# Splitting the queries and keys of both heads once and copying the parts on chip into the doubled layout

## Chip, cores and metric

One core of a Trainium2 chip runs the whole kernel. The metric is the device time of one execution in microseconds.

## What is computed

Three layers follow each other. Only the first is touched by the change; it is cut to its core here, the others are told in a sentence.

```python
# q, k, v: (4 batches, 8 heads, 576 positions, 64), float32
def _attn_ref(q, k, v, tau):
    scores = (1.0 / np.sqrt(64)) * np.matmul(q, k.transpose(0, 1, 3, 2))
    thresh = np.max(scores, axis=-1, keepdims=True) - tau
    scores = np.where(scores >= thresh, scores, -1e9)
    attn = np.exp(scores - np.max(scores, axis=-1, keepdims=True))
    attn = attn / (np.sum(attn, axis=-1, keepdims=True) + 1e-09)
    return np.matmul(attn, v)
```

The heads are then put side by side (512 channels). A mixing layer adds a low-rank product over positions (U, V) and a two-layer channel network with 2048 hidden units. A last layer sends each token to one of eight experts (512 to 1024 to 512); a gate decides whether a token takes a fresh expert or that of the token before it.

## The kernel before

**Splitting.** All large products are made from float32r operands that are split in two: a high part, which is the value rounded by a ScalarE copy, and a low part, which is the value minus the high part.

**Pairs of heads.** The heads are worked on in pairs: 16 pairs, four for each of the four batches. For a pair, `load_pair` makes four tiles: `qs`, `kh`, `kl` (128 partitions by 1216 columns each) and `v`. The 1216 columns hold both heads side by side, with the last 64 positions of the second head placed where the last group of rows needs them. A head has only 64 channels, so the 128 partitions are used twice: `qs` has the high part of the queries on partitions 0 to 63 and the low part on 64 to 127; `kh` has the high part of the keys on both halves, `kl` the low part on both halves. One matmul against `kh` (L293) and one against `kl` (L295) then add up all four products. This is the doubled layout; the host lays out the input tensor with the same data on both halves (`in_qk_dram`, 128 partitions).

**Loading a pair before the change.** For every pair but the first, four pieces are loaded: two of the keys (576 and 640 columns) and two of the queries (608 each), all on 128 partitions (SyncE's DMA queue, L263). ScalarE writes the high part of a piece (L269 for keys, L272 for queries, with the scale), then the low part of the keys is written on 128 partitions (L270) and that of the queries on partitions 64 to 127 alone (L274, VectorE). The engine of L270 is GpSimd for pairs 1 to 7 and VectorE for pairs 8 to 15. The pieces go through a tile `raw` with three buffers; `qs`, `kh`, `kl` and `v` have two buffers each, so the tiles of pair i+1 come free when pair i-1 has been used. The first pair is cut in six pieces so that it can start early.

**Attention of batch 0 alone.** `attention_alone(0)` runs 36 half groups, nine for each pair. A half group is 128 query rows of one head: scores on TensorE (L293, L295), their maximum on VectorE (`peak`, L328), a limit (L332), the exponential on ScalarE (L339), and masking with the row sum on VectorE (L343). Transposes (L391), their evictions on ScalarE (L392), the product with `v` (L410 to L414) and a short chain of mixing steps follow. `load_pair` of the next pair is called in the second group of a pair and is advanced by one step (one `yield` in the loader) for each half group.

**Converting weights.** Beside it, `convert` turns the 64-bit weights of the channel network to float32: a load (L184), a ScalarE cast (L192), a VectorE join (L199) and a store to a DRAM buffer `wdram` (L223). `load_w` reads them back (L609), ScalarE writes their high part (L612) and GpSimd or VectorE the low part (L614).

**Batches 1 to 3.** The attention of batch b is interleaved with the channel network of batch b-1 (`channel`, L630 to L650). Here `load_pair` of the next pair is called as a whole at the start of a pair. After the last attention come the last channel network and the experts.

**Order of work.** Each engine runs its instructions in a fixed order, and so does SyncE's queue, from which all these DMAs are issued: a DMA that has to wait for a semaphore holds up those behind it. The order is laid down at build time by a planner that takes instructions in the order of the program as far as its own estimates say that they are ready.

Of the kernel before, what the change touches and what calls it, by code (L numbers as in the profile page):

```python
# [8 lines left out]
F32 = mybir.dt.float32  # L9
F32R = mybir.dt.float32r  # L10
# [4 lines left out]
AF = mybir.ActivationFunctionType  # L15
ALU = mybir.AluOpType
# [4 lines left out]
B, H, S, D = 4, 8, 576, 64  # L21
# [7 lines left out]
QKW = 1216  # L29
# [54 lines left out]
def attention_channel_moe(ctx, tc, qk, vv, tau, umat, vrep, wch, wgl, wexp, consts, out):  # L84
    nc = tc.nc
    pe, dve, act, pool, sp = nc.tensor, nc.vector, nc.scalar, nc.gpsimd, nc.sync
# [10 lines left out]
    t8 = cp.tile([128, 4], F32, name="t8")  # L97
# [55 lines left out]
    ap = att.enter_context(tc.tile_pool(name="ap", bufs=2, side="right"))  # L153
# [79 lines left out]
    def scalars():  # L233

        sp.dma_start(out=t8[:, 0:1], in_=tau)

        dve.tensor_scalar(out=t8[:, 1:2], in0=t8[:, 0:1], scalar1=NEGTAU, scalar2=0.125, op0=ALU.is_ge, op1=ALU.mult)
        dve.tensor_scalar(out=t8[:, 2:3], in0=t8[:, 1:2], scalar1=0.0, scalar2=BIG, op0=ALU.is_equal, op1=ALU.mult)
        dve.tensor_scalar(out=t8[:, 0:1], in0=t8[:, 0:1], scalar1=0.0, scalar2=t8[:, 2:3], op0=ALU.max, op1=ALU.add)

    def load_pair(b, hp, later=None):

        i = b * NPAIR + hp
        v = ap.tile([128, VW], F32, tag="v", name=f"v{i}")
        qs = ap.tile([128, QKW], F32R, tag="qs", name=f"qs{i}")
        kh = ap.tile([128, QKW], F32R, tag="kh", name=f"kh{i}")
        kl = ap.tile([128, QKW], F32R, tag="kl", name=f"kl{i}")

        cuts = ((0, 0, 128), (1, 0, S), (0, 704, 832), (1, S, QKW), (0, 128, 704), (0, 832, QKW)) if i == 0 else (
            (1, 0, S), (1, S, QKW), (0, 0, 608), (0, 608, QKW))  # L250
        eng = dve if i == 0 or b > 1 else pool
        def steps():
            for n, (kq, c0, c1) in enumerate(cuts):
                c = slice(c0, c1)
                nm = f"raw{i}_{n}"
                if (i, n) == (0, 1):
                    x = mlp.tile([128, S], F32, tag="yr", name=nm, bufs=2)
                elif i == 0 and c1 - c0 == 128:
                    x = mlp.tile([128, 512], F32, tag="wr", name=nm, bufs=WR)
                else:  # L260
                    x = ap.tile([128, 640], F32, tag="raw", name=nm, bufs=3)
                x = x[:, :c1 - c0]
                sp.dma_start(out=x, in_=qk[i][:, kq, c])  # L263
                if (i, n) == (0, 0):
                    scalars()
                if (i, n) == (0, 3):
                    sp.dma_start(out=cst, in_=consts)
                if kq:
                    act.activation(kh[:, c], x, AF.Copy)  # L269
                    eng.tensor_tensor(out=kl[:, c], in0=x, in1=kh[:, c].bitcast(F32), op=ALU.subtract)  # L270
                else:
                    act.activation(qs[:, c], x, AF.Copy, scale=t8[:, 1:2])  # L272
                    lo, hi, xl = qs[64:128, c], qs[64:128, c].bitcast(F32), x[64:128]
                    dve.scalar_tensor_tensor(out=lo, in0=xl, scalar=t8[64:128, 1:2], in1=hi,  # L274
                                             op0=ALU.mult, op1=ALU.subtract)
                yield
            sp.dma_start(out=v, in_=vv[i])

        if later is None:
            for _ in steps():  # L280
                pass
        else:
            later.append(steps())
        return qs, kh, kl, v
# [213 lines left out]
    def attention(b):  # L498
        prev = None
        nxt = load_pair(b, 0)  # L500
        for hp in range(NPAIR):
            inp = nxt
            if hp + 1 < NPAIR:
                nxt = load_pair(b, hp + 1)
            for g in range(5):
                fr = front(b, hp, g, inp)
                yield 1.0
                if prev is not None:
                    yield from with_chain(back(*prev))
                prev = (b, hp, g, inp, fr)  # L510
        yield from with_chain(back(*prev))
        while CHAIN:
            yield link()

    def attention_alone(b):

        pend, debt, loads = [], 0.0, []
        inps = {0: load_pair(b, 0)}
        seq = [(hp, g, h) for hp in range(NPAIR) for g in range(5) for h in range(1 if g == 4 else 2)]
        groups = {}  # L520
# [768 lines left out]
```

## Time and profile before

| | |
|---|---|
| median of 3 runs | 1056.27 us (1054.12 to 1058.85) |
| profiled execution, its own time | 1052.12 us |
| its span, first to last instruction | 1050.4 us |
| mean granted TensorE clock | 0.994 |
| TensorE busy | 1011.7 us (96%) |
| VectorE busy | 714.9 us (68%) |
| ScalarE busy | 576.9 us (55%) |
| GpSimd busy | 133.8 us (13%) |

PE is TensorE's matmul side and PEld its weight loads, DVE is VectorE, ACT is ScalarE, POOL is GpSimd, SP is SyncE, and SPq is its queue. L274 is line 274 of the kernel. The shares are means over stages that differ, so the rows further down go by stretches of the span.

### The profile page before, as it was taken

What the parts mean: (1) busy time and instruction counts of PE and PEld (TensorE: products, weight loads), DVE (VectorE), ACT (ScalarE), POOL (GpSimd) and SP (SyncE); (2) the same over time, 40 slices, a digit from 0 to 9 for tenths busy, and PEclk for the clock granted to TensorE, in tenths of its full rate; (3) what the DMA queues carried; (4) which work ended last, traced back from release to release, by engine and by line L of the source; (5) the groups of instructions that cost most, each with busy time, mean ns of one, the idle gap of its engine ahead of it and who ended that gap; (6) DMA issues with size and microseconds to landing.
All of it is one profiled execution on the core that took longest, in us unless ns stands there. A gap on an engine that the chain in (4) does not pass through costs nothing. (4 is left out here: it accounts for less than half of the span.)

```text
span 1050.4 us, 19186 instructions
## 1 busy us (share of the span) xinstructions
PE 1011.7 (96%) x7081; PEld 896.7 (85%) x7081; DVE 714.9 (68%) x1742; ACT 576.9 (55%) x1216; POOL 133.8 (13%) x114
## 2 busy tenths in 40 slices
PE   8788899999999999999999999999999999999996
PEld 5566789888888999888889988999998988989984
DVE  7889776775776677677767755583367855566673
ACT  6788676674756466474646546422354344455462
POOL 1331032220100000000000000003420321111100
PEclk9999999999999999999999999999999999999998
DMA  6554577763423132142312102353145475456650
GB/s 214 201 157 144 168 251 232 256 217 100 132 71 114 64 93 83 60 132 71 113 55 66 52 31 71 106 201 105 47 160 182 145 262 171 151 189 206 205 181 16
DMA packets 57926, 143.80 MB, mean 137 GB/s; under 512 B 7069, under 2 KB 7837, under 8 KB 57824
## 3 DMA queue, kind: packets, MB, share of 16 engines
q1 hardware_dynamic: 54464, 132.27, 38.5%
q0 software_dynamic: 3360, 10.23, 3.0%
q8 instruction: 57, 0.93, 0.4%
q14 instruction: 45, 0.37, 0.1%
HBM read 124.65 MB, written 18.61 MB: 136 GB/s over the span
## 5 line engine op out<-in xcount | busy, mean ns | idle before, releaser
L630 PE MATMUL l<-uh,w0h 128*128 128x256 f32 (+1 forms) x512 | 158.7, 310 | 0.5 <-DVE L L686 0.2
L647 PE MATMUL l<-hh,w1h 128*128 128x256 f32 (+1 forms) x512 | 156.8, 306 | 0.0
L631 PE MATMUL l<-ul,w0h 128*128 128x256 f32 (+1 forms) x512 | 152.9, 299 | 0.0
L632 PE MATMUL l<-uh,w0l 128*128 128x256 f32 (+1 forms) x512 | 152.7, 299 | 0.0
L649 PE MATMUL l<-hh,w1l 128*128 128x256 f32 (+1 forms) x512 | 152.5, 298 | 0.0
L648 PE MATMUL l<-hl,w1h 128*128 128x256 f32 (+1 forms) x512 | 152.3, 298 | 0.0
L339 ACT ACTIVATE p<-s,st 128x576 f32<-128x576 f32 x144 | 104.3, 741 | 57.0 <-DVE st L328 56.7
L1039 ACT ACTIVATE eh<-ew 128x512 fp32r<-128x512 f32 x160 | 94.3, 628 | 71.6 <-PE el L1155 43.1
L1040 DVE TENSOR_TENSOR el<-ew,eh 128x512 fp32r<-128x512 f32 x160 | 106.6, 692 | 37.7 <-ACT eh L1039 36.3
L343 DVE SCALAR_TENSOR_TENSOR p<-s,st,p 128x576 f32<-128x576 f32 x144 | 114.1, 813 | 11.9 <-ACT p L339 8.3
L328 DVE TENSOR_REDUCE st<-s 128x1 f32<-128x576 f32 x144 | 105.5, 751 | 15.3 <-PE s L295 13.5
L392 ACT ACTIVATE ptt<-tp 128x512 f32<-128x512 f32 (+1 forms) x192 | 91.2, 494 | 39.1 <-PE tp L391 38.1
L293 PE MATMUL s<-kh,qs 128*128 128x288 f32 x320 | 97.3, 323 | 9.7 <-DVE p L343 6.4
L650 DVE TENSOR_TENSOR yT<-l,yT 128x256 f32<-128x256 f32 (+1 forms) x128 | 58.2, 454 | 70.4 <-PE l L649 69.8
L614 POOL TENSOR_TENSOR w1l<-wr,w1h 128x512 fp32r<-128x512 f32 x24 | 32.1, 1359 | 540.8 <-ACT w1h L612 520.9
L630 PEld LDWEIGHTS l<-uh,w0h 128*128 128x128 f32 x512 | 97.4, 190 | 3.9 <-ACT yr L699 2.0
L647 PEld LDWEIGHTS l<-hh,w1h 128*128 128x128 f32 x512 | 97.1, 190 | 2.9 <-issue 2.2
L631 PEld LDWEIGHTS l<-ul,w0h 128*128 128x128 f32 x512 | 97.4, 190 | 0.4
L648 PEld LDWEIGHTS l<-hl,w1h 128*128 128x128 f32 x512 | 97.0, 189 | 0.6
L632 PEld LDWEIGHTS l<-uh,w0l 128*128 128x128 f32 x512 | 97.2, 190 | 0.2
L649 PEld LDWEIGHTS l<-hh,w1l 128*128 128x128 f32 x512 | 96.9, 189 | 0.2 <-issue 0.2
L391 PE MATMUL tp<-cst,p 128*128 128x128 f32 x576 | 92.5, 276 | 3.9 <-ACT ptt L392 3.5
(450 smaller groups left out, 2308.9 us busy)
## 6 DMA issues: line engine op xcount, KB each, us to landing
ew<-in_wexp_dram SPq DMA_DIRECT2D x80, 512.0 KB, 4.5
wr<-wdram SPq DMA_DIRECT2D x128, 256.0 KB, 2.9
cr<-in_wch_dram SPq DMA_DIRECT2D x32, 512.0 KB, 4.9
raw<-in_qk_dram SPq DMA_DIRECT2D x30, 304.0 KB, 3.3
wdram<-w SPq DMA_DIRECT2D x32, 256.0 KB, 3.0
v<-in_vv_dram SPq DMA_DIRECT2D x16, 352.0 KB, 3.3
raw<-in_qk_dram SPq DMA_DIRECT2D x16, 320.0 KB, 3.1
raw<-in_qk_dram SPq DMA_DIRECT2D x17, 288.0 KB, 3.3
```

The lines of the kernel that those rows point to most:

```text
L293: pe.matmul(s["t"][:, h, :288], lhsT=qs[:, qc:qc + 128], rhs=kh[:, k0:k0 + 288], start=(j == 0), stop=False)
L328: dve.tensor_reduce(out=self.st[:, 0, h:h + 1], in_=self.t[h], axis=AX.XY, op=ALU.max, negate=True)
L339: act.activation(self.halves(h), self.t[h], AF.Exp, bias=self.st[:, 0, h:h + 1])
L343: dve.scalar_tensor_tensor(out=p, in0=self.t[h], scalar=self.st[:, 1, h:h + 1], in1=p, op0=ALU.is_ge, op1=ALU.mult, accum_out=self.rvs[:, ...
L630: pe.matmul(pm, lhsT=w1h[:, wk], rhs=uh[:, k, o:o + n], start=(k == 0), stop=False)
L631: pe.matmul(pm, lhsT=w1h[:, wk], rhs=ul[:, k, o:o + n], start=False, stop=False)
L632: pe.matmul(pm, lhsT=w1l[:, wk], rhs=uh[:, k, o:o + n], start=False, stop=(k == 3))
L647: pe.matmul(pm, lhsT=w2h[:, wd], rhs=hh[:, o:o + n], start=(f == f0), stop=False)
L648: pe.matmul(pm, lhsT=w2h[:, wd], rhs=hl[:, o:o + n], start=False, stop=False)
L649: pe.matmul(pm, lhsT=w2l[:, wd], rhs=hh[:, o:o + n], start=False, stop=(f == f0 + 3))
L1039: act.activation(hi, x, AF.Copy)
L1040: dve.tensor_tensor(out=lo, in0=x, in1=hi.bitcast(F32), op=ALU.subtract)
```

## The change

All pairs but the first are loaded by a new generator, `packed`. It loads each of keys and queries once, with the first head on partitions 0 to 63 and the second on 64 to 127 (two DMAs of 64 partitions by 640 columns from `in_qk_dram`). ScalarE writes the high part to a second `raw` tile, the low part is written in place over the loaded tile, both on 128 partitions by 640 columns. Twelve DMAs from SBUF to SBUF, of 64 partitions by 576 or 640 columns, then put these parts into `kh`, `kl` (four each) and `qs` (four). The first pair keeps its six pieces. What `qs`, `kh` and `kl` hold in the end is the same, as are all instructions that read them.

```diff
-        cuts = (...) if i == 0 else ((1, 0, S), (1, S, QKW), (0, 0, 608), (0, 608, QKW))
+        cuts = ((0, 0, 128), (1, 0, S), (0, 704, 832), (1, S, QKW), (0, 128, 704), (0, 832, QKW))
         eng = dve if i == 0 or b > 1 else pool
...
+        def packed():
+
+            for kq in (1, 0):
+                x, hi = (ap.tile([128, 640], F32, tag="raw", name=f"raw{i}_{kq}{t}", bufs=3) for t in "xh")
+                sp.dma_start(out=x[:64], in_=qk[i][:64, kq, 0:640])
+                sp.dma_start(out=x[64:], in_=qk[i][64:, kq, S:QKW])
+                if kq:
+                    act.activation(hi.bitcast(F32R), x, AF.Copy)
+                    eng.tensor_tensor(out=x.bitcast(F32R), in0=x, in1=hi, op=ALU.subtract)
+                    parts = [(t, y, r) for t, y in ((kh, hi), (kl, x)) for r in (0, 64)]
+                else:
+                    act.activation(hi.bitcast(F32R), x, AF.Copy, scale=t8[:, 1:2])
+                    dve.scalar_tensor_tensor(out=x.bitcast(F32R), in0=x, scalar=t8[:, 1:2], in1=hi,
+                                             op0=ALU.mult, op1=ALU.subtract)
+                    parts = [(qs, hi, 0), (qs, x, 64)]
+                yield
+                for t, y, r in parts:
+                    t, c = t[r:r + 64].bitcast(F32), 576 if kq else 640
+                    sp.dma_start(out=t[:, :c], in_=y[:64, :c])
+                    sp.dma_start(out=t[:, c:], in_=y[64:, 640 - QKW + c:])
+                yield
+            sp.dma_start(out=v, in_=vv[i])
+
+        steps = steps if i == 0 else packed
```

## Rows read from the trace of the kernel before

**Rows 1.** Busy time of each engine by stretch of the span.

```profile
core 0: us, PE busy (x) PEld busy (x) DVE busy (x) ACT busy (x) POOL busy (x), PEclk, DMA share, GB/s
27.00:52.00 25.00, 19.59 (x122) 14.30 (x124) 21.60 (x56) 19.25 (x41) 8.80 (x8) 0.93 0.58 196
52.00:75.00 23.00, 20.37 (x141) 14.87 (x139) 20.40 (x53) 19.91 (x43) 5.73 (x5) 1.00 0.51 159
75.00:98.00 23.00, 20.32 (x143) 14.82 (x142) 20.88 (x50) 18.05 (x39) 3.74 (x3) 1.00 0.52 162
...
102.00:146.00 44.00, 39.54 (x280) 34.25 (x280) 32.45 (x75) 31.83 (x71) 10.32 (x9) 0.96 0.59 184
146.00:188.00 42.00, 40.94 (x310) 36.79 (x309) 30.00 (x65) 29.06 (x60) 12.11 (x10) 1.00 0.76 249
...
297.00:461.00 164.00, 162.18 (x1231) 146.51 (x1224) 120.03 (x300) 95.87 (x204) 0.00 (x0) 1.00 0.28 89
```

**Rows 2.** Groups by line and shape from 0 to 110 us, of DVE, ACT and POOL.

```profile
line engine op names shapes xcount | busy us, mean ns | idle before us <-releasers
L343 DVE SCALAR_TENSOR_TENSOR p<-s,st,p 128x576 f32<-128x576 f32 x37 | 29.9, 813 | 4.3 <-ACT p L339 3.9
L274 DVE SCALAR_TENSOR_TENSOR qs<-raw,t,qs 64x608 fp32r<-64x608 f32 x10 | 9.8, 976 | 0.3
...
L272 ACT ACTIVATE qs<-raw,t 128x608 fp32r<-128x608 f32 x10 | 8.1, 814 | 0.6 <-DMA raw<-in_qk_dram 0.6
...
L269 ACT ACTIVATE kh<-raw 128x640 fp32r<-128x640 f32 x6 | 4.4, 737 | 1.6 <-DMA raw<-in_qk_dram 1.6
L269 ACT ACTIVATE kh<-raw 128x576 fp32r<-128x576 f32 x6 | 4.1, 684 | 1.8 <-issue 1.0 <-DMA raw<-in_qk_dram 0.8
...
L270 POOL TENSOR_TENSOR kl<-raw,kh 128x640 fp32r<-128x640 f32 x5 | 8.2, 1646 | 1.2 <-ACT kh L269 1.2
L270 POOL TENSOR_TENSOR kl<-raw,kh 128x576 fp32r<-128x576 f32 x5 | 7.5, 1490 | 16.4 <-ACT kh L269 16.3
```

**Rows 3.** One line's or tile's instructions over the whole span: ns least/median/most.

```profile
L274 DVE SCALAR_TENSOR_TENSOR qs<-raw,t,qs x34: 351/851/2095, 4.4 to 564.1; 64x608 fp32r<-64x608 f32 x30, 64x128 fp32r<-64x128 f32 x2, 64x576 fp32r<-64x576 f32 x1, 64x384 fp32r<-64x384 f32 x1
...
L199 DVE SCALAR_TENSOR_TENSOR w<-cr,top x32: 673/683/1733, 31.9 to 242.5; 128x512 int32<-128x512 int32 x32
```

**Rows 4.** Timeline of POOL and DVE around 75 and 99 us (start, duration).

```profile
75.59 2.92 POOL L270 TENSOR_TENSOR kl<-raw,kh 128x576 fp32r<-128x576 f32 x2 [2.95 <-ACT kh L269]
...
77.06 2.10 DVE L274 SCALAR_TENSOR_TENSOR qs<-raw,t,qs 64x608 fp32r<-64x608 f32 x1
...
99.04 3.39 POOL L270 TENSOR_TENSOR kl<-raw,kh 128x576 fp32r<-128x576 f32 x2 [0.58 <-ACT kh L269]
...
99.51 1.49 DVE L199 SCALAR_TENSOR_TENSOR w<-cr,top 128x512 int32<-128x512 int32 x1
```

**Rows 5.** DMA issues: KB each, median us from issue to landing.

```profile
raw<-in_qk_dram SPq DMA_DIRECT2D x17, 288.0 KB, 3.3
ydram<-yr SPq DMA_DIRECT2D x16, 256.0 KB, 3.2
ydram<-yr SPq DMA_DIRECT2D x4, 128.0 KB, 2.4
```

**Rows 6.** The stores out of tile w: us to landing, least/median/most.

```profile
DMA to landing us min/median/max: 2.0/3.0/5.5
```

**Rows 7.** Timeline around the loading of pair 1: SPq, ACT, PE.

```profile
9.71 0.33 SPq L263 DMA_DIRECT2D raw<-in_qk_dram  x1
...
11.62 0.86 SPq L263 DMA_DIRECT2D raw<-in_qk_dram  x2
...
13.59 0.67 ACT L269 ACTIVATE kh<-raw 128x576 fp32r<-128x576 f32 x1
...
28.38 0.40 PE L293 MATMUL s<-kh,qs 128*128 128x288 f32 x1 [0.35 <-DVE p L343]
```

**Rows 8.** Pair 2: last low part, first scores; batch 0: last scores; pair 6.

```profile
41.79 0.85 DVE L274 SCALAR_TENSOR_TENSOR qs<-raw,t,qs 64x608 fp32r<-64x608 f32 x1
...
54.55 0.40 PE L293 MATMUL s<-kh,qs 128*128 128x288 f32 x1
...
97.25 0.30 PE L295 MATMUL s<-kl,qs 128*128 128x288 f32 x1
...
152.76 0.85 DVE L274 SCALAR_TENSOR_TENSOR qs<-raw,t,qs 64x608 fp32r<-64x608 f32 x1 [0.19 <-ACT qs L272]
...
188.67 0.38 PE L293 MATMUL s<-kh,qs 128*128 128x288 f32 x1
```

**Rows 9.** Waits of SP's queue from 0 to 100 us: total, times, longest.

```profile
SPq L223 <- DVE w L199: 22.3, 5, 7.5
SPq L263 <- DVE qs L274: 12.8, 6, 3.6
SPq L263 <- POOL kl L270: 12.1, 7, 3.0
```

**Rows 10.** A converted weight on its way: store issue, load issue, low part, first use.

```profile
128.97 0.32 SPq L223 DMA_DIRECT2D wdram<-w  x1
...
132.34 0.32 SPq L609 DMA_DIRECT2D wr<-wdram  x1
...
133.83 1.30 POOL L614 TENSOR_TENSOR w0l<-wr,w0h 128x512 fp32r<-128x512 f32 x1 [1.23 <-ACT w0h L612]
...
137.87 0.36 PE L630 MATMUL l<-uh,w0h 128*128 128x256 f32 x1
```

More of the change, by code (lines that the diff above doesn't have):

```diff
@@ L247, in load_pair @@
         kl = ap.tile([128, QKW], F32R, tag="kl", name=f"kl{i}")
-        cuts = ((0, 0, 128), (1, 0, S), (0, 704, 832), (1, S, QKW), (0, 128, 704), (0, 832, QKW)) if i == 0 else (
-            (1, 0, S), (1, S, QKW), (0, 0, 608), (0, 608, QKW))
+        cuts = ((0, 0, 128), (1, 0, S), (0, 704, 832), (1, S, QKW), (0, 128, 704), (0, 832, QKW))
         eng = dve if i == 0 or b > 1 else pool
@@ L255, in steps @@
                 nm = f"raw{i}_{n}"
-                if (i, n) == (0, 1):
+                if n == 1:
                     x = mlp.tile([128, S], F32, tag="yr", name=nm, bufs=2)
-                elif i == 0 and c1 - c0 == 128:
+                elif c1 - c0 == 128:
                     x = mlp.tile([128, 512], F32, tag="wr", name=nm, bufs=WR)
@@ L263, in steps @@
                 sp.dma_start(out=x, in_=qk[i][:, kq, c])
-                if (i, n) == (0, 0):
+                if n == 0:
                     scalars()
-                if (i, n) == (0, 3):
+                if n == 3:
                     sp.dma_start(out=cst, in_=consts)
```

## The prediction

> **What bounds the kernel now.** I read the busy time by stretch first, then the loader's own groups, then single instructions around the loads.
>
> By stretch [rows 1] the span falls in two. From about 102 us on, TensorE is the bound: 162.2 of 164 us busy between 297 and 461 us, 40.9 of 42 between 146 and 188. Work taken from other engines there can give back only the holes, 1.8 us and 1.1 us in these two stretches. Before 98 us it is different. From 27 to 98 us DVE is busy for 21.6 + 20.4 + 20.9 = 62.9 of 71 us (89%), ACT for 57.2 (81%), PE for 60.3 (85%, with room). In this stretch a half group passes DVE, ACT and DVE again, and DVE has least room: it sets the pace, together with the hand-overs to ACT. The DVE group L343 shows 4.3 us of idle time, 3.9 of it behind ACT's exponential [rows 2]. So what the change does to DVE, and to a lesser degree to ACT, in the first 110 us is what can shorten the run. Five pairs (1 to 5) are split in that time: ten query pieces of L274 and ten POOL subtractions [rows 2].
>
> **The change part by part.**
>
> *Query low parts on DVE (removed and replaced).* Two L274 of 64x608 at 0.851 us median [rows 3] become one of 128x640. Using 128 partitions in place of 64 costs nothing: L343, of the same kind with as many columns but on 128 partitions, takes 0.813 us for 576 [rows 2]. With some 32 more columns I take 0.88 us. Saved for a pair: 1.70 - 0.88 = 0.82 us, for five pairs 4.1 us.
>
> *High parts on ACT.* Four copies, 0.684 + 0.737 + 2 x 0.814 = 3.05 us [rows 2], become two: 0.737 for the keys and about 0.84 for the queries (0.814 with 32 columns more, at 53 ns for 64 columns as between the two key pieces). Saved: 1.47 us for a pair, 7.3 us for five.
>
> *Key low parts.* On POOL 1.490 + 1.646 = 3.14 us become 1.65 [rows 2]; 1.49 us are saved for a pair. POOL is idle most of the time, so that by itself is worth nothing. But two DVE instructions that ran beside L270 took 2.10 us where the median is 0.851, and 1.49 us where it is 0.683 [rows 3, 4]: 2.1 us lost to DVE. With half of the POOL work I take half of that back, 1.0 us; ends 0 and 2.1. In batches 2 and 3 the same subtraction is DVE's and gets cheaper by about half, in a stretch that PE bounds: nothing.
>
> So DVE gets 5.1 us in the stretch that it paces. How much becomes time? At least nothing (the pieces may already sit in DVE's idle time, 8.1 of 71 us), at most all 5.1. I take half, **-2.6 us**: the splits can be placed freely, so a part of them fills waits, but with 89% busy not all can. ACT's 7.3 us I count as nothing in the forecast; a rival counts them.
>
> *Loads from the input.* Four DMAs of 128 partitions become four of 64, with 64 x 640 x 4 bytes = 160 KB each; the loaded bytes of a pair fall from 1.19 to 0.63 MiB. Off the path.
>
> *Copies from SBUF to SBUF (added).* Twelve for a pair, 180 in all, each 144 or 160 KB on 64 partitions; 1.78 MiB a pair. No row shows such a copy. One issue costs SP 0.43 us (two in 0.86 [rows 7]), so 5.2 us of SP time for a pair. The landing: the nearest rows are stores out of SBUF, 2.4 us for 128 KB from 64 partitions and 3.2 us for 256 KB from 128 [rows 5], and 2.0 to 5.5 us with a median of 3.0 for the stores of w [rows 6]. I take 3.0 with ends 2.0 and 5.5. In those two rows of ydram half the data takes three quarters of the time, so two halves one after the other would be dearer than one whole, but they are issued 0.43 us apart and overlap. The Trainium skill speaks against this layout: in "SBUF — State Buffer", section "Can I just issue two DMAs to hit both halves?", it says that two DMAs on the two halves of the partitions run hardly faster than one after the other, and in "The DMA port swizzle" that 64 partitions reach half of the ports. By that rule the twelve copies would move at the rate of half the ports, and the estimate from its 218 GB/s is 8.6 us of transfer for a pair; no row here shows it.
>
> *Is the new chain early enough?* The new order is load, ACT, POOL, copy, land, and for the queries once more, with a second wait in between: `raw` has three buffers, so the high part of the queries needs a buffer that the key copies have freed. For pair 1, with ACT starting at 13.6 us as now [rows 7]: high part done at 14.3, POOL at 15.9. The four high copies are issued by 16.0 and land at 16.0 + L; then ACT 0.84, DVE 0.88, four copies 1.7, and the last lands at 19.4 + 2L, plus up to 1.6 us if ACT and DVE are each busy with one instruction. With L = 3.0 that is 25.4 to 27.0 us, with 5.5 it is 30.4 to 32.0, with 2.0 it is 23.4. The pair's first scores run at 28.38 [rows 7]. So the price is 0 to 3.6 us; I take **+0.5**. Pairs from 2 on have cover: the last low part of pair 2 is done at 42.64 and its scores start at 54.55, for pair 6 it is 153.61 and 188.67 [rows 8]. The two landings and the issues fit in 11.9 us. They even start sooner, since the split no longer waits for the old `kh` to be free; only the copies do. Without that cover a pair would cost one landing, 3.0 us.
>
> *SP's queue.* Behind a waiting copy stand the loads and stores of the converted weights; they in turn feed ACT's casts (L192) and the low parts (L614). SP already waits much, 22.3 us in all for the join and 12.1 us behind POOL's `kl` up to 100 us [rows 9], so its own time is not short. After 110 us I take 0 with ends -2 and +2, the size of the holes of PE [rows 1].
>
> **Sum.** 1052.12 (profiled execution) - 2.6 + 0.5 = 1050.0 us. The median of the runs is 4.15 us above the profiled execution, so the forecast against it is **1054.2 us**, 0.2% faster. A measurement of this kernel tells about 0.5% from no change, 5.3 us, so I call this no difference.
>
> **The rivals.**
>
> *Hidden anyway.* The splits already fill waits, and the gain of DVE turns into idle time: 1056.3, or 1056.8 with the late start of pair 1. For it: 8.1 us of DVE idle time between 27 and 98 us. Against it: DVE is the busiest engine there.
>
> *Both engines count.* A half group needs DVE, ACT and DVE in turn, and ACT is also busy for 81%; a piece on either delays the exponential. Then all 5.1 us of DVE count and half of ACT's 7.3: 8.8 us, 1052.12 - 8.8 = 1043.3, or 1047.5 beside the median. For it: DVE's waits for the exponential [rows 2]. Against it: PE has 5.4 + 2.6 + 2.7 = 10.7 us of idle time from 27 to 98 us [rows 1], so PE itself would soon bound the stage.
>
> *SP's queue holds up the weights (slower).* A copy of a low part waits at the head of SP's queue until POOL is done (1.65 us), and the query copies wait for a landing (3.0): 4.65 us in which nothing behind them is issued. A converted weight has little room: its low part ends at 133.83 + 1.30 = 135.13 us and PE uses it at 137.87 [rows 10], 2.7 us. Each of pairs 2 to 5, loaded while weights are converted, would then cost 4.65 - 2.7 = 1.95 us, 7.8 us in all: 1050.0 + 7.8 = 1057.8, or 1062.0 beside the median. It decides from a hold of 2.7 us on, if planner and chip disagree on when the copies are ready. For it: the holds already there [rows 9] and a DMA share of 0.76 between 146 and 188 us [rows 1], which lengthens landings. Against it: the low parts of pairs 2 to 5 fall before the weights are needed. The rule on halves quoted above would bring the same result, since it lengthens every landing.
>
> *The change not doing what it says* is not among them: fewer and wider instructions are in the diff itself.
>
> **How the numbers follow.** Forecast 0.37, hidden anyway 0.18, both engines 0.24, SP's queue 0.21. Forecast and hidden lie within 0.5%: same 0.55; faster by over 0.5% (below 1051.0) 0.24; slower (above 1061.6) 0.21. The range takes in the values of all rivals and some of their spread: 1046 to 1064.
>
> **What would show it.** In the profile after: one L274-like instruction of 128x640 for a pair at about 0.88 us, ACT copies of 640 columns at 0.74 and 0.84, POOL subtractions of 1.65 us; DVE busy 4 to 5 us less up to 110 us and the last scores of batch 0 some 2 to 3 us earlier than 97.5 [rows 8]; first scores of pair 1 near 28; copies that land in 2.4 to 4 us; unchanged busy time and about the same holes of PE after 110 us. I am wrong if the end of the first stage moves by over 5 us either way, if DVE or PE wait for `qs`, `kh` or `kl`, if PE has new holes before L630 and L647, or if the granted clock falls in a new hole.

## The result and the profile after

The changed kernel takes 1066.87 us (median of 4 runs, 1065.62 to 1067.93) beside 1055.9 us for the kernel before (4 runs, 1054.12 to 1058.85). The ratio is 1.0100 with a 95% interval of 1.0078 to 1.0122: about 11 us, or 1.0%, slower. The forecast was 1054.2 us, and the range ended at 1064.

The profiled execution took 1065.62 us, its span is 1063.8 us, and the granted clock is 0.994 as in the profile of before, so the loss isn't one of clock. First the page of after, its lines of busy time and the group of the matmul with `w0l` (L655, before L632; lines behind the loader have moved by 23):

```profile
PE 1019.3 (96%) x7080; PEld 898.0 (84%) x7081; DVE 697.0 (66%) x1719; ACT 562.5 (53%) x1186; POOL 123.8 (12%) x107
...
L655 PE MATMUL l<-uh,w0l 128*128 128x256 f32 (+1 forms) x512 | 152.3, 299 | 3.5 <-POOL w0l L637 3.3
```

The relief came: VectorE is busy 697.0 us in place of 714.9, ScalarE 562.5 in place of 576.9, GpSimd 123.8 in place of 133.8. It was not turned into time. A matmul lasts as long as before (299 ns for this group). Busy time by stretch, the columns of [rows 1]:

```profile
27.00:52.00 25.00, 20.63 (x130) 13.58 (x131) 18.35 (x48) 17.25 (x38) 4.25 (x5) 1.00 0.74 206
52.00:75.00 23.00, 18.83 (x132) 14.41 (x131) 16.91 (x48) 18.12 (x39) 2.83 (x2) 1.00 0.67 175
75.00:98.00 23.00, 20.66 (x140) 14.70 (x139) 18.56 (x51) 16.86 (x38) 2.20 (x2) 1.00 0.78 216
```

From 27 to 98 us VectorE has 53.8 us of work where it had 62.9 [rows 1], and it stands idle instead. Not all of the difference is relief: by 110 us the queries of three pairs have been split in place of five [rows 2], so some of that work has only been put off. TensorE does no more than before. How far it falls behind is best counted in matmuls, since a matmul that starts late by less than its own length leaves no idle time. Three stretches, 0 to 110, 110 to 188 and 188 to 297 us (PE busy and its count, granted clock, DMA share, GB/s), of before and then of after:

```profile
0.00:110.00 110.00, 93.37 (x589) 0.98 0.58 185
110.00:188.00 78.00, 73.92 (x547) 0.98 0.66 210
188.00:297.00 109.00, 106.75 (x812) 1.00 0.51 162
```

```profile
0.00:110.00 110.00, 93.14 (x578) 1.00 0.76 206
110.00:188.00 78.00, 71.30 (x515) 0.98 0.77 231
188.00:297.00 109.00, 103.63 (x764) 1.00 0.76 221
```

After is 11 matmuls behind by 110 us, 32 more by 188 and 48 more by 297: 91, and at 164 us for 1231 matmuls [rows 1] that is 12.1 us. It agrees with the first scores of pair 8, at 309.79 us in place of 297.23. From there on the distance stays, up to 13.4 us between the two spans; these two profiles lie a little further apart than the medians. The last scores of batch 0 run at 101.74 us in place of 97.25 [rows 8], but the first matmul of the channel network runs at 117.7 us in both. Nearly nine tenths of the loss come after 110 us, where I had put 0, and what falls behind there is the first layer of the channel network: from 110 to 188 us 152 of its matmuls run (L653 to L655) in place of 199.

Two waits of after tell of two places. Up to 110 us VectorE's maximum waits for scores (total, times, longest; before, then after). Between 110 and 290 us TensorE waits for a low part of weights, which it never did before:

```profile
DVE st L328 <- PE s L295: 4.8, 9, 1.2
```

```profile
DVE st L351 <- PE s L318: 16.2, 14, 5.3
```

```profile
PEld l L655 <- POOL w0l L637: 5.2, 7, 1.2
...
PE l L655 <- POOL w0l L637: 3.3, 6, 0.9
```

The second wait is small beside the loss: 3.3 us before matmuls, 5.2 us before their weight loads, while the 80 matmuls lost after 110 us are worth 10.7 us at the rate above. The rest isn't traced to a wait.

**Place 1: pairs that start late.** Pair 1, in the timeline of after (start, duration, engine, line):

```profile
20.49 0.60 SPq L283 DMA_DIRECT2D raw_0x<-in_qk_dram  x1
...
28.34 0.85 ACT L289 ACTIVATE raw_0h<-raw_0x,t 128x640 fp32r<-128x640 f32 x1
...
31.05 0.55 SPq L297 DMA_DIRECT2D qs<-raw_0x  x1
...
34.98 0.40 PE L316 MATMUL s<-kh,qs 128*128 128x288 f32 x1
...
35.81 0.76 DVE L351 TENSOR_REDUCE st<-s 128x1 f32<-128x576 f32 x1 [5.27 <-PE s L318]
```

The second half of the queries is loaded behind the eight key copies, and the first scores run at 34.98 us in place of 28.38 [rows 7]. Pair 2 has the same shape, the whole chain from its first load on:

```profile
32.28 0.49 SPq L282 DMA_DIRECT2D raw_1x<-in_qk_dram  x1
...
40.24 0.73 ACT L285 ACTIVATE raw_1h<-raw_1x 128x640 fp32r<-128x640 f32 x1
...
41.11 1.55 POOL L286 TENSOR_TENSOR raw_1x<-raw_1x,raw_1h 128x640 fp32r<-128x640 f32 x1 [9.87 <-ACT raw_1h L285]
...
45.39 0.60 SPq L297 DMA_DIRECT2D kl<-raw_1x  x1
46.03 0.60 SPq L282 DMA_DIRECT2D raw_0x<-in_qk_dram  x1
...
54.27 0.84 ACT L289 ACTIVATE raw_0h<-raw_0x,t 128x640 fp32r<-128x640 f32 x1
...
57.04 0.52 SPq L297 DMA_DIRECT2D qs<-raw_0x  x1
...
60.63 0.40 PE L316 MATMUL s<-kh,qs 128*128 128x288 f32 x1
```

From the load at 32.28 us to the scores at 60.63 us it is 28.4 us, while the pair before it took 26.2 us in the old kernel (28.38 to 54.55) [rows 7, 8]. Two rounds of load, split, copy and landing follow each other, and the queries' round begins only when the key copies have been issued. Such a chain, one pair ahead, is longer than what it hides behind.

**Place 2: weights that come late.** Between 145.5 and 149 us, the low part of a weight and the matmul that reads it:

```profile
147.24 1.28 POOL L637 TENSOR_TENSOR w0l<-wr,w0h 128x512 fp32r<-128x512 f32 x1 [2.34 <-PE s L318]
...
148.57 0.39 PE L655 MATMUL l<-uh,w0l 128*128 128x256 f32 x1 [0.55 <-POOL w0l L637]
```

In before the low part was done 2.7 us ahead of its use [rows 10]. The conversion itself has fallen behind: its 17th store (L223) is issued at 163.1 us before and at 176.6 us after. Its way back has grown longer still. The load that reads a stored weight back (L609, now L632) stands in the same queue; for the seventh weight, before and after:

```profile
141.51 0.44 SPq L223 DMA_DIRECT2D wdram<-w  x1
...
148.72 1.37 SPq L609 DMA_DIRECT2D wr<-wdram  x2
```

```profile
146.74 0.32 SPq L223 DMA_DIRECT2D wdram<-w  x1
...
178.09 1.69 SPq L632 DMA_DIRECT2D wr<-wdram  x2
```

Between this store and its load stand 5 other DMAs before and 29 after, among them all twelve copies of a pair; these 29 take 15.2 us to issue, and on the way the queue waits 13.4 us for semaphores. For the 3rd to the 16th weight it is 31 DMAs before and 170 after, and the median time from the store's issue to the load's is 3.0 us before and 13.3 us after.

What both places share is SyncE's queue. Summed over the rows of the trace, up to 110 us it spends 24.5 us on issuing 64 DMAs before, and 54.4 us on 102 after.

### The profile page after: what moved, and what is told of

It is laid out like the page before. It is cut to its first block, busy times and chain, and to the rows that moved or that the text cites. A ratio compares the mean times of both kernels' runs of the same rounds, so it can differ in the third digit from the quotient of the medians.

```text
span 1063.8 us, 19421 instructions
## 1 busy us (share of the span) xinstructions
PE 1019.3 (96%) x7080; PEld 898.0 (84%) x7081; DVE 697.0 (66%) x1719; ACT 562.5 (53%) x1186; POOL 123.8 (12%) x107
## 4 chain that ended last, share of the span: by engine, by line
PE 75%; DVE 7%; ACT 6%; DMA 5%; issue 4%; SPq 1%; POOL 1%; POOLq 0%; ACTq 0%; DVEq 0%
PE l L670 6%; PE l L653 6%; PE l L671 6%; PE l L672 6%; PE l L655 6%; PE l L654 5%; PE po L433 5%; PE el L1131 3%; PE tp L414 3%; PE el L1133 3%; PE el L1132 3%; PE s L316 3%; PE el L1178 3%; PE el L1176 3%; PE el L1177 3%
## 5 line engine op out<-in xcount | busy, mean ns | idle before, releaser
L653 PE MATMUL l<-uh,w0h 128*128 128x256 f32 (+1 forms) x512 | 158.8, 311 | 1.1 <-DVE L L709 0.5
L655 PE MATMUL l<-uh,w0l 128*128 128x256 f32 (+1 forms) x512 | 152.3, 299 | 3.5 <-POOL w0l L637 3.3
L366 DVE SCALAR_TENSOR_TENSOR p<-s,st,p 128x576 f32<-128x576 f32 x144 | 114.3, 814 | 13.5 <-ACT p L362 9.4
L653 PEld LDWEIGHTS l<-uh,w0h 128*128 128x128 f32 x512 | 97.2, 190 | 5.6 <-ACT yr L722 2.0
L655 PEld LDWEIGHTS l<-uh,w0l 128*128 128x128 f32 x512 | 96.5, 189 | 5.4 <-POOL w0l L637 5.2
```

The lines of the kernel that those rows point to most:

```text
L366: dve.scalar_tensor_tensor(out=p, in0=self.t[h], scalar=self.st[:, 1, h:h + 1], in1=p, op0=ALU.is_ge, op1=ALU.mult, accum_out=self.rvs[:, ...
L653: pe.matmul(pm, lhsT=w1h[:, wk], rhs=uh[:, k, o:o + n], start=(k == 0), stop=False)
L655: pe.matmul(pm, lhsT=w1l[:, wk], rhs=uh[:, k, o:o + n], start=False, stop=(k == 3))
```

## The experiments

Three explanations stood against each other: the late chains of batch 0 (chain); SyncE's queue, held by issues and by copies that wait, so that the conversion lags and weights come late (queue); and the bytes and landings of the new traffic itself (bytes: 163.0 MB moved in place of 143.8). The expectations call the first A2 or rival C, the second theory A or rival D, and the third rival B; each spells out what it means. Ratios are to the kernel before on the same chip. "SP" is the issuing time on SyncE's queue up to 110 us and from 110 to 250 us, summed from its rows: 24.5 and 33.5 us before, 54.4 and 63.7 after.

### Where it is: one batch at a time

```diff
-        steps = steps if i == 0 else packed
+        steps = packed if i and b == 0 else steps   # likewise b == 1, b > 1, b > 0
```

> Only pairs 1 to 3 (the rest of batch 0) are loaded the new way; pairs 4 to 15 as before. Theory A, SP's queue in order holds up the converted weights in batch 1 and the late pairs of batch 0 cost some 4 us on top: about +2 to +4 us against the kernel before. Rival B, each pair pays the same for its twelve copies, 11/15 = 0.73 us: +2.2 us. Rival C, the late first scores of pairs 1 to 3 (6 to 7 us each) are the whole loss: +11 us.

> Only pairs 4 to 7 (batch 1, beside which the weights are converted) are loaded the new way. Theory A: +6 to +9 us, and the low parts of the weights end after the matmuls of their step have begun. Rival B: 4 x 0.73 = +2.9 us. Rival C: 0 to +1 us.

> Only pairs 8 to 15 (batches 2 and 3, all weights converted by then) are loaded the new way, with all their 96 copies. Theory A: nothing, -1 to +1 us. Rival B: 8 x 0.73 = +5.9 us. Rival C: 0.

> The new loader for pairs 4 to 15 only; pairs 1 to 3 are loaded as before. Theory A (the loss is made in batch 0, by pairs whose last query copy lands too late, and by SyncE's queue held while weights are converted): the sum of the two runs with batch 1 alone (+2.0) and batches 2 and 3 alone (-0.8), so +1 us, 1055 to 1059; in the first 110 us VectorE's waits for scores stay near the 4.8 us of before. Rival D (the late weights of batch 1 come from batch 1's own copies, added to those of later batches): +7 to +8 us, and waits of PE for w0l of about 3 us between 110 and 290 us.

Measured: pairs 1 to 3 alone 1.0088 (1.0068 to 1.0109), 1064.94 us beside 1055.62; batch 1 alone 1.0017 (0.9996 to 1.0037); batches 2 and 3 alone 0.9993 (0.9974 to 1.0013); batches 1 to 3 together 1.0010 (0.9984 to 1.0035). That is +9.3, +1.8, -0.7 and +1.0 us. Theory A had put most of the loss on batch 1 and was wrong; rival C was nearest for batch 0, and rival B, an equal price for each pair, is out, since 96 copies in batches 2 and 3 cost nothing. The loss needs batch 0, and the parts add up: 0.88 + 0.17 - 0.07 = 0.98%. None of the four runs has a wait for `w0l` of TensorE. Late weights need the copies of batch 0 and of batch 1 together, and the rows of the queue tell why. With batch 0 alone the conversion lags as much as in the change (17th store at 176.9 us), but its stores are loaded back after 2.8 us in the median. With batches 1 to 3 the way back takes 9.6 us, but the conversion lags less (170.7 us), and the least room between a low part and its use is 0.4 us, where it was 2.0 before. The change has both.

That the sum fits doesn't make the parts alike. With batch 0 alone the loss is taken earlier: the last scores of batch 0 run at 107.02 us, and the first matmul of the channel network at 129.3 us in place of 117.7. Its scores of pair 2 start at 64.30 us, TensorE stands idle before that, and the clock falls (three stretches of 3 us, the columns as above):

```profile
57.00:60.00 3.00, 2.29 (x18) 1.00 0.22 46
60.00:63.00 3.00, 1.06 (x6) 0.91 1.01 254
63.00:66.00 3.00, 2.96 (x9) 0.52 0.87 228
```

Behind the hole 9 matmuls run in 3 us where 18 ran before it, at 0.52, which is close to the lower level of 1.2 GHz. In the profile of after the clock holds at 1.00 from 57 to 66 us. By 188 us this run is 37 + 64 = 101 matmuls behind, and then 3 more:

```profile
0.00:110.00 110.00, 92.83 (x552) 0.95 0.71 197
110.00:188.00 78.00, 69.08 (x483) 0.93 0.66 207
188.00:297.00 109.00, 106.72 (x809) 1.00 0.62 185
```

So the copies of batch 0 are enough for 9 us; in the full change they cost less (11 matmuls by 110 us), and the rest comes later. How much of the 9 us is clock isn't shown. The four runs have a median granted clock of 0.989 beside 0.992 before, and this profile, 14.1 us above that of before, shows more than the medians' 9.3. But the profile of the control further down, which loses no time in its median, has such a stretch too: 0.51, close to the lower level again, from 39 to 45 us.

### Which copies

```diff
+        def queries():   # or keys(); the other tensor is loaded in two pieces as before
...
+            for y, r in ((hi, 0), (x, 64)):
+                sp.dma_start(out=t[:, :640], in_=y[:64, :640])
+                sp.dma_start(out=t[:, 640:], in_=y[64:, 64:])
```

> Queries alone are loaded the new way, ahead of the keys: one round, four copies; the keys are loaded in the doubled layout as before. Theory A2: the chain has one round and fits in the lead, -3 to +2 us. Rival B or D, by the number of copies: 4/12 of 11, +3.7 us.

> Keys alone are loaded the new way, eight copies; the queries come in two pieces in the doubled layout as before. Theory A2: one round, so most of the loss is gone, 0 to +4 us. Rival B or D, by the number of copies: 8/12 of 11, +7.3 us.

Measured: queries alone, four copies, 1.0000 (0.9978 to 1.0023), SP 38.4 and 42.0 us. Keys alone, eight copies, 1.0046 (1.0022 to 1.0071), SP 49.2 and 48.7 us; neither waits for `w0l`. Both parts together cost 1.0%: more than their sum. The queries' copies bring VectorE's gain on the low parts (L290 in place of two L274), and the time is the same: whatever that gain is worth, no more is left of it beside its copies than 0.2% can tell.

### SyncE's queue without any copy

Stores that nobody reads are added to the kernel before, at the places of the copies: twelve of 64 partitions for a pair; the same for pairs 1 to 3 alone; or three whole tiles of 128 partitions with the same bytes. Nothing else waits for them.

```diff
+                if i and n in (1, 3):
+                    for m, (t, r) in enumerate(...):      # kh, kl, qs; r = 0 and 64
+                        sp.dma_start(out=spare[o:o + 64, :w], in_=t[:, :w])
+                        sp.dma_start(out=spare[o + 64:o + 128, :QKW - w], in_=t[:, w:])
...
+                        sp.dma_start(out=spare[o:o + 128, :], in_=t.bitcast(F32))   # whole tiles
```

> The kernel before with twelve extra DMAs for each of pairs 1 to 15, of the same shapes, out of the finished kh, kl and qs into a spare DRAM buffer that nobody reads: they hold SP and move bytes, but no scores wait for them; the splits are the old ones. Theory A2: 0 to +3 us. Rival D: as much as the changed kernel or more, +8 to +12 us, with the weights' low parts late. Rival B: +11 us.

> The kernel before with the twelve spare stores (64 partitions, nobody reads them) for pairs 1 to 3 alone. Theory A (SyncE's queue held during batch 0 delays the conversion of weights, and this comes out as late weights in batch 1): most of the +7 to +8 us of the run with spare stores for all pairs, so +5 to +8. Rival D (the queue held during batch 1 itself makes the weights late): +0 to +2, and no wait for w0l.

> The kernel before with three added stores for each pair but the first, of the whole tiles kh, kl and qs (128 partitions by 1216 columns) to a DRAM buffer that nobody reads; the same bytes as in the run with twelve spare stores of 64 partitions (+7 to +8 us). If the number of issues on SyncE's queue is what costs (theory A): SP's issuing time from 0 to 110 us rises by about 12 x 0.4 = 5 us in place of 25, the late weights vanish and the time is +0 to +3 us. If the bytes cost (rival B: 1.8 MiB more traffic for each pair delays the weights' own transfers): +7 us again, with PE waiting some 3 us for w0l between 110 and 290 us.

Measured: twelve halves 1.0075 (1.0048 to 1.0102), SP 50.0 and 61.5 us; for pairs 1 to 3 alone 1.0025 (1.0010 to 1.0039), SP 47.1 and 30.9; three whole tiles 0.9992 (0.9968 to 1.0016), SP 36.6 and 43.1. Matmuls by stretch, with twelve halves and with three whole tiles:

```profile
0.00:110.00 110.00, 95.39 (x586) 0.98 0.75 227
110.00:188.00 78.00, 69.64 (x505) 1.00 0.80 247
188.00:297.00 109.00, 103.56 (x770) 1.00 0.76 239
```

```profile
0.00:110.00 110.00, 92.91 (x581) 0.97 0.77 257
110.00:188.00 78.00, 73.55 (x552) 1.00 0.78 251
188.00:297.00 109.00, 106.97 (x807) 1.00 0.64 214
```

With twelve halves the deficit is 3, 42 and 42: after 110 us the pattern of after, without a copy, without a new chain and without a change to any split. The wait comes back as well (first the run with halves):

```profile
PEld l L640 <- POOL w0l L622: 4.8, 8, 0.9
...
PE l L640 <- POOL w0l L622: 2.8, 7, 0.6
```

With whole tiles there is no such wait, at the same bytes and with the DMA engines as busy (0.77 and 0.78). The weights' loads land no later with halves (4.0 us in the median up to 250 us) than with whole tiles (4.7). Bytes are out; what costs is SyncE's queue: the way back of a weight takes 14.5 us in the median with halves and 4.0 with whole tiles. It has two parts that these runs don't separate, the time of the issues and the place in the queue that the planner gives each DMA. Theory A had expected +5 to +8 us from the halves of pairs 1 to 3 and was wrong there too (+2.6 us, no wait for `w0l`). The rows of both show why three stores hold it so much less (timeline; whole tiles, then halves):

```profile
30.97 0.42 SPq L280 DMA_DIRECT2D spare<-kh  x1
36.45 0.38 SPq L280 DMA_DIRECT2D spare<-kl  x1
46.61 0.33 SPq L280 DMA_DIRECT2D spare<-qs  x1
```

```profile
18.74 0.54 SPq L283 DMA_DIRECT2D spare<-kl  x1
19.33 0.59 SPq L282 DMA_DIRECT2D spare<-kl  x1
19.97 0.59 SPq L283 DMA_DIRECT2D spare<-kl  x1
```

A store of 608 KB on 128 partitions is issued in 0.32 to 0.42 us, one of 144 or 160 KB on 64 partitions mostly in 0.54 to 0.59. Up to 110 us that makes 5.2 us for 15 stores against 25.4 us for 46.

### Loads first

```diff
+            made = {}
+            for kq, hs in ((1, "xh"), (0, "x")):      # both loads ahead of the key split and copies
+                made[kq] = [ap.tile([128, 640], F32, tag="raw", ..., bufs=3) for t in hs]
+                sp.dma_start(out=made[kq][0][:64], in_=qk[i][:64, kq, 0:640])
+                sp.dma_start(out=made[kq][0][64:], in_=qk[i][64:, kq, S:QKW])
```

> As the changed kernel in all pairs, but the loads of the queries stand ahead of the splits and copies of the keys, so that they are no longer issued behind eight copies. Theory A: the last copy of pair 1 is issued some 5 us sooner (25 in place of 31 us), SP stands still for fewer us between the key and the query copies, and the loss falls from +11 to about +3 to +7 us. Rival B, as many copies and bytes: +11 us still. Rival C: the pairs of batch 0 start on time, and the loss falls to about 0.

Measured: 1.0140 (1.0111 to 1.0169), +14.8 us, worse than all three theories had it. Pair 1 starts nearly on time (29.55 us), pair 2 at 60.93 us all the same, and the weights are late again (3.3 us). In its timeline pair 2's first half key is issued at 33.44 us and the other half only at 37.83 us, behind stores of converted weights (L223, 35.82 and 37.45 us) that wait 1.9 and 0.8 us for VectorE. I read it so: a shorter chain for one pair is of no use while its pieces and the conversion wait for each other in one queue.

### Other queues

```diff
-                    sp.dma_start(out=t[:, :c], in_=y[:64, :c])
+                    pool.dma_start(out=t[:, :c], in_=y[:64, :c])     # or act. for the four query copies
...
-            sp.dma_start(out=raw[:, 1:1 + 4 * m], in_=src[:, c0:c0 + m].bitcast(U16))
+            act.dma_start(out=raw[:, 1:1 + 4 * m], in_=src[:, c0:c0 + m].bitcast(U16))   # L184, and L223 too
```

> The changed kernel with its twelve copies of a pair issued from GpSimd's queue in place of SP's; loads, splits, bytes and the three raw buffers stay. Theory A2, formed after the first four runs: in batch 0 the loader's own chain (two rounds of load, split, copies and landing through three buffers) is longer than its lead, and the first scores of a pair wait for the last copy of the queries; the chain is the same here, so +5 to +12 us. Rival D, SP's queue is what loses the time, since weights and loads stand behind waiting copies: SP is free of them, 0 to +3 us. Rival B, copies cost by number and bytes: +11 us.

> The changed kernel, with the four query copies of a pair issued from ScalarE's queue, and the eight key copies left on SyncE's. The copies, bytes and landings are the same. Theory A: SyncE's queue has 2.4 us less for a pair and no stand-still behind a query's low part; this would be about the run with key copies alone, +4 to +6 us, plus what 20 issues on ScalarE up to 110 us cost its exponentials (0 to 6 us). Rival B: +11 and more.

> The changed kernel, with the loads (L184) and stores (L223) of the weights' conversion issued from ScalarE's queue, so that they no longer stand behind the copies on SyncE's queue. Theory A has two parts. Late weights: they vanish (PE's waits for w0l below 0.5 us in place of 3.3), worth 5 to 7 us of the +11. Late pairs in batch 0: SyncE's queue is relieved of some 40 issues up to 110 us, so the last query copy of pairs 2 and 3 lands 1 to 3 us sooner. Sum: +2 to +6 us over the kernel before, if the added issues on ScalarE (about 0.05 to 0.4 us each) cost nothing. Rival B (bytes and transfers, not the queue): +11 as in the changed kernel. If ScalarE's added issues or waits for the join hold up the exponentials: +11 or more, with VectorE waiting for ScalarE's p.

> The kernel before with the loads (L184) and stores (L223) of the conversion issued from ScalarE's queue: the control for the changed kernel with the same move (+22). If the move itself is what costs there (ScalarE waits at the head of its queue for the join, and the conversion falls behind): +10 to +20 us, and the copies then add 2 to 12. If it is free: 0 to +2, and the move and the copies hurt only together.

Measured: all copies from GpSimd's queue 1.0424 (1.0376 to 1.0472); query copies from ScalarE's queue 1.0158 (1.0118 to 1.0198); the conversion moved to ScalarE's queue in the changed kernel 1.0211 (1.0171 to 1.0251), and in the kernel before 1.0146 (1.0125 to 1.0166). My expectation of +2 to +6 us for the third was wrong, and so was that of +4 to +12 for the second; for the first none of the three theories, which ended at +12, comes near +45. The fourth tells why for the third: the move alone costs 1.5%. ScalarE then waits at L192 for VectorE's join (14.3 us up to 300 us), and the last store of the conversion is issued at 263.0 us in place of 243.2 us. Against that control the copies cost 1.0211 / 1.0146 = 1.0064, with no late `w0l`: less than 1.0100, as the queue would have it, but in kernels so changed I take it as a hint only. For the second: ScalarE issues the four copies of a pair in 0.48 to 0.62 us each, among its exponentials, and pair 2 starts at 62.81 us; its runs also have a lower granted clock, 0.981 in the median beside 0.989 before. From GpSimd's queue the key copies land late: the median up to 110 us is 2.5 us for the 144 KB and 7.4 for the 160 KB copies of the high part, 8.1 and 5.2 us for those of the low part.

None of the three moves gained anything. The Trainium skill says in "Trainium Kernel Development and Optimization", section "Key Constraints", that DMAs from several engines run on the same DMA engines and that issuing from several saves only the issuing sequencer's time. Here the engine that took the issues over paid for that saving: 14.3 us of ScalarE's waits in the fourth run.

### Fewer copies

The keys' high and low part lie in one tile, so that one DMA copies both: four key copies for a pair in place of eight. Space for it: `WR` 5 in place of 6 and a smaller warm-up tile, which the control has too. In the run with the keys alone the shared tile has a buffer of its own, and the queries' `raw` has two buffers in place of three.

```diff
+            raw = ap.tile([128, 2, 640], F32, tag="raw", name=f"raw{i}_{kq}", bufs=2)
...
+                    for r in (0, 64):
+                        t = khl[r:r + 64].bitcast(F32)
+                        sp.dma_start(out=t[:, :, :576], in_=raw[:64, :, :576])
+                        sp.dma_start(out=t[:, :, 576:], in_=raw[64:])
```

> Keys alone by the new way, like the run with eight key copies (+4.9 us), but high and low part lie in one tile, so that one DMA of 64 partitions copies both: four key copies for a pair in place of eight, the same bytes. For the space, WR is 5 in place of 6 and the warm-up tile has 448 columns; the kernel before with these two edits runs beside it. Theory A (each issue costs SyncE's queue 0.6 us): 4 x 0.6 = 2.4 us of SP less for a pair, and +0 to +2 us over that control. Rival B (the bytes and the landings cost): +4 to +6 us over the control, as with eight copies.

> The whole change with eight copies for a pair in place of twelve (a key's high and low part in one copy), and two raw tiles of 1280 columns, so that the load of the queries doesn't wait for key copies. WR 5 and the smaller warm-up tile as in the control. Theory A: half of the issues that were added are gone up to 110 us (38 becomes about 18), the chain of a pair loses one of its two waits, and pairs 1 to 3 start 2 to 5 us sooner than in the changed kernel: +2 to +5 us over the control in place of +11, and no wait of PE for w0l of over 1 us. Rival B (bytes, landings): +9 to +12 over the control.

> The kernel before with WR at 5 in place of 6 and the warm-up tile of 448 columns: the control for the two runs with merged copies. 0 to +3 us; more if a buffer less for the weights that are read back makes PE wait for w0l or w1l.

Measured: the control 0.9993 (0.9966 to 1.0020); keys alone 1.0013 (0.9991 to 1.0035), SP 47.7 and 47.3 us; the whole change with eight copies 1.0113 (1.0078 to 1.0148), SP 52.9 and 55.7. Over the control that is +0.2% and +1.2%. The first can't be told from eight copies (+0.46%), the second, expected at +2 to +5 us, is no better than the change: the theory of the number of issues fell. The issue rows and the landings of the last kernel (timeline, then DMA groups up to 110 us) show why:

```profile
20.11 0.92 SPq L296 DMA_DIRECT2D kh<-raw  x1
21.08 1.33 SPq L297 DMA_DIRECT2D kh<-raw  x1
```

```profile
kh<-raw SPq DMA_DIRECT2D x8, 320.0 KB, 4.9
kh<-raw SPq DMA_DIRECT2D x8, 288.0 KB, 5.3
```

A copy of two parts takes SyncE 0.60 to 1.36 us to issue, and the query copies, whose shape is that of the change, now take 0.81 us in the median in place of 0.54. So the issues of 32 copies up to 110 us last 27.2 us, where 44 copies of the change last 25.3. TensorE waits for `w0l` in this run again (3.0 us), and pair 2's two half keys are loaded at 31.04 and 39.03 us, with a store of weights between them. Why issues lengthen isn't settled. Shape and neighbour both count: in the trace of after up to 250 us, with SyncE idle for over 0.3 us before it, a DMA of 128 partitions takes 0.32 us to issue in the median and one of 64 partitions 0.49; right behind one of its own kind it is 0.43 and 0.59.

Set side by side, the time on the queue up to 110 us orders the kernels, though only roughly:

| kernel | SP to 110 us | SP 110 to 250 us | ratio | `w0l` late |
|---|---|---|---|---|
| before | 24.5 | 33.5 | 1 | no |
| batches 1 to 3 | 35.5 | 54.4 | 1.0010 | no |
| whole spare stores | 36.6 | 43.1 | 0.9992 | no |
| batch 1 alone | 36.4 | 53.2 | 1.0017 | no |
| queries alone | 38.4 | 42.0 | 1.0000 | no |
| batch 0 alone | 47.0 | 34.0 | 1.0088 | no |
| spare halves, batch 0 | 47.1 | 30.9 | 1.0025 | no |
| merged keys alone | 47.7 | 47.3 | 1.0013 | no |
| keys alone | 49.2 | 48.7 | 1.0046 | no |
| spare halves | 50.0 | 61.5 | 1.0075 | 2.8 us |
| merged, whole | 52.9 | 55.7 | 1.0113 | 3.0 us |
| the change | 54.4 | 63.7 | 1.0100 | 3.3 us |
| loads first | 54.4 | 59.5 | 1.0140 | 3.3 us |

Below 40 us nothing is lost that the intervals can tell, whatever follows; late weights come where both columns are high. The way back of a weight parts the kernels more sharply: the median time from store to load is 13.3 to 14.7 us in the four that have late weights, and 2.8 to 9.7 us in all others. Batch 0 alone stands out: spare halves take as much of the queue in batch 0 and cost 0.25%, so most of its 0.88% goes with the late chains and with what of the clock belongs to them.

## Why the prediction was wrong

- *VectorE paces the first stage, TensorE the rest* [rows 1]. The second half held, and so did the first as a reading of before. But the relief could only turn into time if nothing else ended last. VectorE did 9.1 us less work from 27 to 98 us, some of it put off, and up to 110 us waited 16.2 us for scores in place of 4.8. The last scores of batch 0, expected 2 to 3 us earlier, came 4.5 us later.
- *Sizes of the compute steps.* Right: the query low part takes 0.88 us (0.88 said), ScalarE's high parts 0.74 and 0.83 (0.74 and 0.84), GpSimd's 1.55 (1.65):

```profile
L286 POOL TENSOR_TENSOR raw_1x<-raw_1x,raw_1h 128x640 fp32r<-128x640 f32 x4 | 6.2, 1550 | 68.4 <-DMA wr<-wdram 44.8 <-ACT raw_1h L285 23.6
L290 DVE SCALAR_TENSOR_TENSOR raw_0x<-raw_0x,t,raw_0h 128x640 fp32r<-128x640 f32 x3 | 2.6, 880 | 0.1
```

- *One issue costs SP 0.43 us.* Mis-sized: 0.46 to 0.61 us for copies and for the 64-partition loads (one took 1.31). I had taken it from DMAs of 128 partitions [rows 7], and costed the loads' issue at nothing. For a pair it is about 7 us of copies, not 5.2, and SP's issuing time more than doubled. I costed that time only for the chain of pair 1, not for those who queue behind it.
- *Landing 3.0 us.* Near: up to 110 us the medians are 3.4 (`kh`), 4.1 to 4.2 (`kl`), 2.5 to 2.7 (`qs`); the 160 KB loads take 4.4 to 4.8.
- *Pair 1 late by 0 to 3.6 us, +0.5 taken.* Mis-sized: 6.6 us late. I let the queries' split follow at once; in fact their second load was placed behind all eight key copies, and ScalarE's step at 28.34 us came 3.7 us after that load had landed.
- *Pairs from 2 on have 11.9 us of cover.* This is the step that failed first. I compared the landings with the time between the last split and the first scores of before [rows 8], as if the splits stayed where they were. But the chain has its own second round: the queries' load, split and copies all start behind the key copies. Pairs 2 and 3 start at 60.63 and 83.73 us in place of 54.55 and 76.25.
- *SP's queue after 110 us: 0, ends -2 and +2.* This is the step that carries the most: 80 of the 91 matmuls are lost there. I weighed it by TensorE's holes, that is by what the queue cost before, and not by what it would cost with twice the time on it. In its place the runs showed weights that come back 13.3 us after their store in place of 3.0, a first layer of the channel network that falls behind, and the same pattern (+0.75%) from stores that nobody reads.
- *The rival "SP's queue holds up the weights"* named the right mechanism, 1062.0 us at a chance of 0.21. Its price was too low, since it counted one hold of 4.65 us for each of four pairs; the queue's delay adds up instead over batches 0 and 1 (17th store 13.5 us late), and comes out as late weights in batch 1. Its statement against itself, that the low parts of pairs 2 to 5 fall before the weights are needed, missed the point: what they hold back is the way of a weight that is needed later. I counted the holds, but not what the copies put between a weight's store and its load.
- *The rule on the two halves* (the Trainium skill, "SBUF — State Buffer", "Can I just issue two DMAs to hit both halves?"). By it only one transfer over all 128 partitions reaches all ports, so each copy would land later than its bytes suggest. The runs agree: 320 KB from 64 partitions land in 4.9 us, about as late as whole tiles of 608 KB on 128 partitions (4.3 to 5.7 us). But the landings aren't what decided: spare halves that nobody waits for cost three quarters of the loss.

What stays open: how the 11 us divide between the two places. Batch 0 alone loses 0.88% in part with a lower clock, the spare stores 0.75% without any late chain, and the two can't simply be added, since the whole is 1.0%. Also open is how much of the way back is issuing time and how much the order that the planner laid down, and why an issue is dearer on 64 partitions than on 128. None of these kernels beats the one before.

## What to carry over

When a change replaces compute by DMAs, cost the issuing queue as an engine of its own: its busy time, what stands behind each waiting DMA, above all between a store and the load that reads it back, and whose deadline that is. Spare stores that added 25.5 us to this queue up to 110 us and 28.0 from 110 to 250 cost 0.75%, while the same bytes in a quarter of the DMAs cost nothing. Lay a new chain out in full, round by round with the queue's order, and compare its length with the pair it hides behind, not with the slack that the old chain left. An engine that paces a stage gives time back only if the next thing to be late, here the loader, stays early.

## What was unexpected of the hardware

- SyncE's time to issue a DMA doesn't follow the bytes: 0.32 to 0.42 us for whole tiles of 608 KB on 128 partitions, mostly 0.45 to 0.61 us for 144 or 160 KB on 64, 0.60 to 1.36 us for 288 or 320 KB on 64 in two pieces. It also goes by the DMA ahead of it: one of 128 partitions right behind one of 64 takes 0.55 us in the median, in place of 0.32 alone. Single issues in the trace of after reach 1.8 us.
- The spread of the kernel before, 1052.3 to 1061.2 us from run to run on four chips and 1056.3 to 1066.8 on a fifth, goes largely with the granted clock: 1052.4 us at 0.994, 1055.0 at 0.990, 1059.6 at 0.988 (with exceptions, as 1058.7 at 0.991). A profile of 1052.12 us was thus one of the quickest, and that is why kernels are compared by their medians here.
